# Rounding float64 weights block by block between the products that read them, in five VectorE passes instead of seven

## Chip, cores and metric

One core of one Trainium2 chip. The metric is the device time of one execution in microseconds (us).

## The reference, cut to what matters

Two steps follow each other. The first is a gated linear recurrence over 768 tokens for 4 batches of 8 heads of 48 channels. The second takes its output as `x` (4 x 768 x 384), mixes it with a two-dimensional Fourier transform, normalises it and sends it through a feed-forward layer whose weights arrive as float64.

```python
f = 1.0 / (1.0 + np.exp(-f_logit))
for t in range(S):
    state = f[:, :, t, :, None] * state + np.einsum('bhd,bhe->bhde', k[:, :, t], v[:, :, t])
    y[:, :, t] = np.einsum('bhd,bhde->bhe', q[:, :, t], state)
# ... x = y with the heads side by side: (B, S, H*D)
u = x + np.real(np.fft.fft(np.fft.fft(x, axis=1), axis=2))
un = (u - u.mean(-1)) / np.sqrt(u.var(-1) + 1e-06)        # shortened
return u + np.maximum(un @ w_ch1, 0.0) @ w_ch2            # w_ch1 384x1536, w_ch2 1536x384
```

## The kernel before

The attention runs in 16 units (two heads each, four units to a batch), the feed-forward layer in four batches of two halves. A unit's data lie in one of three buffers; its load into a buffer can only begin when the unit that held it is done. The float64 weights come as pairs of 32-bit words and are rounded to float32 on the chip, in 24 blocks of 128 x 384 (twelve of w1, twelve of w2), by integer arithmetic:

```python
def single(i, dst, src):                        # one block
    raw = p2.tile([128, n, 2], U32, tag="unT", name=f"raw{i}")
    # ... load; lo, hi are its two words; pow2, tail, tailf are three tiles of the pool ph1 (14 slots)
    vec.tensor_scalar(bits, hi, 3, 0x3FFFFFF8, ALU.logical_shift_left, ALU.bitwise_and)
    vec.scalar_tensor_tensor(bits, hi, 0xC0000000, bits, ALU.bitwise_and, ALU.bitwise_or)
    vec.scalar_tensor_tensor(bits, lo, 29, bits, ALU.logical_shift_right, ALU.bitwise_or)
    vec.tensor_scalar(tailb, lo, 0x1FFFFFFF, None, ALU.bitwise_and)
    vec.tensor_scalar(pow2b, bits, 0xFF800000, None, ALU.bitwise_and)
    nc.scalar.activation(tailf, tailb, AF.Copy, scale=2.0 ** -52)
    nc.gpsimd.tensor_tensor(tailf, tailf, pow2, ALU.mult)
    nc.gpsimd.tensor_tensor(dst, dst, tailf, ALU.add)
    vec.tensor_scalar(tailb, hi, 0x7FF00000, None, ALU.bitwise_and)
    vec.scalar_tensor_tensor(dst, tailb, float(897 << 20), dst, ALU.is_ge, ALU.mult)

# ... the states of a unit, in outputs(): one product and four dependent operations
nc.vector.tensor_tensor(st, ds, T.unsqueeze(2).to_broadcast([R, NCH - 1, D]), ALU.mult)
for c in range(1, NCH - 1):
    nc.vector.scalar_tensor_tensor(st[:, c], st[:, c - 1], T[:, c:c + 1], ds[:, c], ALU.mult, ALU.add)

# ... the feed-forward layer, in fnet(): the hidden activations take twelve of the 14 slots of ph1
for m in range(NF):                             # NF = 12
    for kt in range(3):
        nc.tensor.matmul(pp[:, :3 * 128], lhsT=w1[:, kt, m * 128:(m + 1) * 128], rhs=unT[:, kt], ...)
    h = ph1.tile([128, 3 * 128], F32, tag="h1", ...)
    nc.scalar.activation(h, pp[:, :3 * 128], AF.Relu)
for i in range(3):
    for m in range(NF):
        nc.tensor.matmul(po[:, :DM], lhsT=h1[m][:, i * 128:(i + 1) * 128], rhs=w2[:, m], ...)

# ... run(): at each tick every active unit goes one step on, then two steps of the work "behind" follow
run(attention, STEP, [weights()])               # the 24 blocks stand first in that work
```

Of the kernel before, what the change touches and what calls it, by code (L numbers as in the profile page):

```python
# [8 lines left out]
U32 = mybir.dt.uint32  # L9
# [8 lines left out]
HIGH = 22.0  # L18
X_MIN = -24.0
# [3 lines left out]
def kernel(  # L23
# [29 lines left out]
    p2 = ctx.enter_context(tc.tile_pool(name="p2", bufs=2))  # L53
    p3 = ctx.enter_context(tc.tile_pool(name="p3", bufs=4))
# [14 lines left out]
    deep = fixed([128, B * HP], "deep")  # L69
# [17 lines left out]
    for t in qkf_t:  # L87
        nc.vector.memset(t[32:64, 0:2], 0.0)
        nc.vector.memset(t[32:64, 2], 30.0)
# [7 lines left out]
    def load_unit(u):  # L97
        b, hp = divmod(u, HP)
        t = qkf_t[u % 3]
        for r in range(2):  # L100
            nc.sync.dma_start(out=t[ROWS[r]], in_=qkf[b, hp, r])
        vt = p3.tile([128, NCH, 2 * D], F32, tag="v", name=f"v{u}")
        nc.sync.dma_start(out=vt, in_=v[b, hp])
        return vt
# [9 lines left out]
    for t in at_t:  # L114
        nc.gpsimd.memset(t, 0.0)
# [4 lines left out]
    def single(i, dst, src):  # L120


        n = dst.shape[-1]
        raw = p2.tile([128, n, 2], U32, tag="unT", name=f"raw{i}")
        nc.sync.dma_start(out=raw.rearrange("p n w -> p (n w)"), in_=src)
        lo, hi = raw[:, :, 0], raw[:, :, 1]
        pow2 = ph1.tile([128, n], F32, tag="h1", name=f"pow2_{i}")
        tail = ph1.tile([128, n], F32, tag="h1", name=f"tail{i}")
        tailf = ph1.tile([128, n], F32, tag="h1", name=f"tailf{i}")
        bits, pow2b, tailb = (t.bitcast(U32) for t in (dst, pow2, tail))  # L130
        vec = nc.vector

        vec.tensor_scalar(bits, hi, 3, 0x3FFFFFF8, ALU.logical_shift_left, ALU.bitwise_and)
        vec.scalar_tensor_tensor(bits, hi, 0xC0000000, bits, ALU.bitwise_and, ALU.bitwise_or)
        vec.scalar_tensor_tensor(bits, lo, 29, bits, ALU.logical_shift_right, ALU.bitwise_or)

        vec.tensor_scalar(tailb, lo, 0x1FFFFFFF, None, ALU.bitwise_and)
        vec.tensor_scalar(pow2b, bits, 0xFF800000, None, ALU.bitwise_and)  # L138
        nc.scalar.activation(tailf, tailb, AF.Copy, scale=2.0 ** -52)  # L139
        nc.gpsimd.tensor_tensor(tailf, tailf, pow2, ALU.mult)  # L140
        nc.gpsimd.tensor_tensor(dst, dst, tailf, ALU.add)  # L141
        vec.tensor_scalar(tailb, hi, 0x7FF00000, None, ALU.bitwise_and)
        vec.scalar_tensor_tensor(dst, tailb, float(897 << 20), dst, ALU.is_ge, ALU.mult)  # L143

    def weights():
        pairs = [(w1[:, kt], w_ch1[kt * 128:(kt + 1) * 128]) for kt in range(3)]
        pairs += [(w2[:, m], w_ch2[m * 128:(m + 1) * 128]) for m in range(NF)]
        i = 0
        for dst, src in pairs:
            if src.dtype == F32:  # L150
                nc.sync.dma_start(out=dst, in_=src)
                yield
                continue
            words = src.bitcast(U32)
            for o in range(0, dst.shape[-1], 384):
                single(i, dst[:, o:o + 384], words[:, 2 * o:2 * (o + 384)])
                i += 1
                yield

    def attention(u, x_all):  # L160




        t = qkf_t[u % 3]
        Q, K, g = t[:R, 0], t[:R, 1], t[:R, 2]
        AT = at_t[u % 2]
        L = p2.tile([128, S], F32, tag="gk", name=f"L{u}")[:R]
        G = p2.tile([128, S], F32, tag="wq", name=f"G{u}")[:R]
        W = p2.tile([128, S], F32, tag="wk", name=f"W{u}")[:R]  # L170
        at = lambda a, i, c: a.rearrange("p (c t) -> p c t", t=C)[:, c, i]
        nc.vector.tensor_scalar(g, g, X_MIN, None, ALU.max)
        nc.scalar.activation(L, g, AF.Exp, scale=-1.0)
        nc.scalar.activation(L, L, AF.Ln, bias=1.0)  # L174
        nc.vector.tensor_tensor_scan(G, L, bound[:R], 0.0, ALU.add, ALU.min)  # L175
        nc.vector.tensor_reduce(deep[:R, u:u + 1], at(G, C - 1, slice(0, NCH)), mybir.AxisListType.X, ALU.max)

        T = p2.tile([128, NCH - 1], F32, tag="te", name=f"te{u}")[:R]
        nc.vector.tensor_tensor(T, at(G, C - 1, slice(0, NCH - 1)), at(L, 0, slice(1, NCH)), ALU.add)
        nc.scalar.activation(W, G, AF.Exp)  # L180
        nc.scalar.activation(G, G, AF.Exp, scale=-1.0)
        nc.scalar.activation(T, T, AF.Exp, scale=-1.0, bias=low[:R])
        nc.gpsimd.tensor_tensor(W, W, K, ALU.mult)  # L183
        nc.vector.tensor_tensor(Q, Q, G, ALU.mult)  # L184
        yield

        for h in range(2):
            ps = ps_a.tile([128, 2, 512], F32, tag="sc", name=f"sc{u}_{h}")
            for i in range(NCH // 2):
                o = (h * NCH // 2 + i) * C  # L190
                for s in range(2):
                    for r in range(2):
                        nc.tensor.matmul(ps[64 * s:64 * s + 64, r, i * C:(i + 1) * C],  # L193
                                         lhsT=W[ROWS[r], o + 64 * s:o + 64 * s + 64],
                                         rhs=Q[ROWS[r], o:o + C], start=True, stop=True)
            for r in range(2):
                half = slice(h * NCH // 2, (h + 1) * NCH // 2)
                nc.vector.copy_predicated(  # L198
                    AT[:, r, half],
                    causal.bitcast(U32).unsqueeze(1).to_broadcast([128, NCH // 2, C]),  # L200
                    ps[:, r, :NCH // 2 * C].rearrange("p (c t) -> p c t", t=C))
        yield
        yield from outputs(u, x_all, AT, Q, W, T, True)

    def attention_by_blocks(u, x_all):
# [25 lines left out]
        wq = p2.tile([128, S], F32, tag="wq", name=f"wq{u}")[:R]  # L231
        wk = p2.tile([128, S], F32, tag="wk", name=f"wk{u}")[:R]
        gk = p2.tile([128, S], F32, tag="gk", name=f"gk{u}")[:R]
# [89 lines left out]
        yield from outputs(u, x_all, AT, Q, K, T, False)  # L323

    def outputs(u, x_all, AT, Q, K, T, from_start):
# [12 lines left out]
        ds = ps[:R, 0, :(NCH - 1) * D].rearrange("p (c e) -> p c e", e=D)  # L338
        for c in range(NCH - 1):
            for r in range(2):  # L340
                nc.tensor.matmul(ds[FILL[r], c], lhsT=kT[:, c, FILL[r]], rhs=vt[:, c, r * D:(r + 1) * D],  # L341
                                 start=True, stop=True)
        st = p2.tile([128, NCH - 1, D], F32, tag="st", name=f"stt{u}")[:R]
        if from_start:
            nc.vector.tensor_tensor(st, ds, T.unsqueeze(2).to_broadcast([R, NCH - 1, D]), ALU.mult)
            ds = st
        else:
            nc.vector.tensor_copy(st[:, 0], ds[:, 0])
        for c in range(1, NCH - 1):
            nc.vector.scalar_tensor_tensor(st[:, c], st[:, c - 1], T[:, c:c + 1], ds[:, c],  # L350
                                           ALU.mult, ALU.add)
# [9 lines left out]
        for c in range(1, NCH):  # L361
            for r in range(2):
                nc.tensor.matmul(y[ROWS[r], c * C:(c + 1) * C], lhsT=st[ROWS[r], c - 1],  # L363
# [27 lines left out]
    def fnet(b, x):  # L391
# [42 lines left out]
        def mixed(name, rows, n):  # L434
            mix = ps_f.tile([128, 512], F32, tag="f", name=name)
            for T in range(3):
                nc.tensor.matmul(mix[:rows.stop - rows.start, :n], lhsT=zz[:, T, rows], rhs=cd[:, T, :n],  # L437
                                 start=(T == 0), stop=(T == 2))
            return mix

        mid = mixed(f"mid{b}", slice(HS, HS + 1), DM)
        row = p1.tile([128, DM], F32, tag="row", name=f"row{b}")
        nc.vector.tensor_tensor(row[0:1], mid[0:1, :DM], x[0:1, 3], ALU.add)
# [17 lines left out]
        for half in range(2):  # L461
# [11 lines left out]
            for m in range(NF):  # L473
                pp = ps_f.tile([128, 512], F32, tag="f", name=f"up{b}_{half}_{m}")
# [8 lines left out]
            for i in range(3):  # L483
                c = 3 * half + i
                po = ps_f.tile([128, 512], F32, tag="f", name=f"po{b}_{c}")
                for m in range(NF):
                    nc.tensor.matmul(po[:, :DM], lhsT=h1[m][:, i * 128:(i + 1) * 128], rhs=w2[:, m],  # L487
# [7 lines left out]
    def run(unit_of, step, behind):  # L495
        left, xs_of, active, done = [HP] * B, {}, [], 0
        u = tick = 0
        while u < B * HP or active or behind:
            if u < B * HP and tick % step == 0:
# [3 lines left out]
                active.append((b, unit_of(u, xs_of[b])))  # L503
                u += 1
            for b, unit in list(active):
                if next(unit, active) is active:
                    active.remove((b, unit))
                    left[b] -= 1
                    if not left[b]:
                        behind.append(fnet(b, xs_of.pop(b)))  # L510
# [5 lines left out]
    run(attention, STEP, [weights()])  # L516
# [3 lines left out]
    nc.vector.tensor_reduce(most[:R], deep[:R], mybir.AxisListType.X, ALU.max)  # L520
# [6 lines left out]
    with tc.If(again > 0):  # L527
        v_of.update({i: load_unit(i) for i in range(3)})
        run(attention_by_blocks, 3, [])
# [69 lines left out]
```

## Time and profile before

The median of the three runs taken first is 728.3 us (727.58 to 731.77). The profiled span is 725.6 us (that run read 727.62). I cut it at two places: where the first feed-forward product ("up") of the first batch starts, and where the second output product of that batch ("po_1") is added to x.

| stretch of before | us | TensorE busy | VectorE busy | GpSimd busy | mean clock |
|---|---|---|---|---|---|
| to the first up product | 205.4 | 109.1 | 163.2 | 89.2 | 0.69 |
| from there to the addition of po_1 | 45.9 | 45.9 | 15.8 | 9.9 | 0.98 |
| the rest | 474.3 | 449.8 | 93.4 | 34.1 | 0.98 |

The row of the first stretch is one line of the view by windows; its columns are the window, its length, then busy us and count for PE, PEld, DVE, ACT and POOL, then the clock, the DMA share and GB/s:

```profile
0.00:205.40 205.40, 109.14 (x1044) 73.52 (x1044) 163.23 (x320) 63.14 (x111) 89.23 (x78) 0.69 0.47 118
```

VectorE is 79% busy here.

### The profile page before, as it was taken

The page shows a single profiled execution, that of the slowest core. Times are in us where ns is not written, and L with a number is a line of the kernel's source. Part 1 is how long each engine was busy: PE and PEld are TensorE (multiplying, and loading weights), DVE is VectorE, ACT ScalarE, POOL GpSimd, SP SyncE. Part 2 cuts the span into 40 slices and gives each one's busy share as a digit, 9 for nine tenths or more (in the row PEclk, how much of TensorE's full clock was granted, in tenths as well). Part 3 has the DMA queues.
Part 4 walks back from the last instruction along what each step waited for, and adds up shares of the span by engine and source line. Part 5 has one row for each costly group of instructions (what it writes and reads, how often), then busy time and mean ns, then how long its engine had stood idle before and what let it go on. Part 6 is the DMA issues. An engine that isn't in the chain of part 4 may idle for free.

```text
span 725.6 us, 8305 instructions
## 1 busy us (share of the span) xinstructions
PE 604.9 (83%) x3402; PEld 370.1 (51%) x3402; DVE 272.5 (38%) x541; ACT 167.7 (23%) x317; POOL 133.2 (18%) x109
## 2 busy tenths in 40 slices
PE   0853446157799999999999999987999998999995
PEld 0642334034456665666556655554555553555553
DVE  5777788888861421126922100144000004001000
ACT  2521322124261132122531120122202101210200
POOL 3225545644220400021400000120000010000001
PEclk9875555659789999999999999997999999899999
DMA  9835444242320030313310000000000000000000
GB/s 169 225 85 130 127 105 129 85 114 82 65 50 1 23 77 1 77 39 74 67 25 11 23 0 12 22 1 1 0 23 11 1 22 11 1 0 33 0 12 27
DMA packets 11182, 35.56 MB, mean 49 GB/s; under 512 B 1600, under 2 KB 3776, under 8 KB 9472
## 3 DMA queue, kind: packets, MB, share of 16 engines
q1 hardware_dynamic: 10368, 32.58, 18.1%
q0 software_dynamic: 768, 2.36, 0.8%
q8 instruction: 29, 0.48, 0.3%
q14 instruction: 17, 0.14, 0.1%
HBM read 30.22 MB, written 4.72 MB: 48 GB/s over the span
## 4 chain that ended last, share of the span: by engine, by line
PE 49%; DVE 4%; ACT 1%; DMA 1%; POOL 1%; issue 0%; ACTq 0%; DVEq 0%; POOLq 0%
PE up L476 20%; PE po L487 19%; PE z L424 3%; PE pt L469 1%; PE y L363 1%; PE y L358 1%; PE mix L437 1%; PE sc L193 1%; DVE bs L453 1%; DMA out_dram<-x,place 1%; PE mid L437 1%; PE ds L341 1%; POOL eo L400 1%; PE st L334 1%; PE yt L374 0%
## 5 line engine op out<-in xcount | busy, mean ns | idle before, releaser
L476 PE MATMUL up<-unT,w 128*128 128x384 f32 x576 | 195.3, 500 | 2.3 <-ACT unT L470 2.3
L487 PE MATMUL po<-w,h 128*128 128x384 f32 x576 | 188.8, 487 | 0.0
L476 PEld LDWEIGHTS up<-unT,w 128*128 128x128 f32 x576 | 111.2, 195 | 81.7 <-issue 5.8
L487 PEld LDWEIGHTS po<-w,h 128*128 128x128 f32 x576 | 108.9, 190 | 75.1 <-issue 0.5
L489 DVE TENSOR_TENSOR x<-po,x 128x384 f32<-128x384 f32 x24 | 13.4, 558 | 292.0 <-PE po L487 292.0
L479 ACT ACTIVATE h<-up 128x384 f32<-128x384 f32 x96 | 47.0, 490 | 136.3 <-PE up L476 136.3
L386 POOL DMA_INDIRECT out_dram<-x,place x12 | 13.1, 1090 | 331.3 <-DVE x L489 324.5
L363 PE MATMUL y<-qkf,stt 48*48 48x128 f32 x320 | 34.2, 325 | 46.7 <-DVE stt L350 36.4
L193 PE MATMUL sc<-qkf,W 48*64 48x128 f32 x768 | 39.1, 336 | 32.9 <-DVE qkf L184 24.2
L183 POOL TENSOR_TENSOR W<-W,qkf 112x768 f32<-112x768 f32 x16 | 29.9, 1866 | 117.2 <-ACT W L180 117.2
L193 PEld LDWEIGHTS sc<-qkf,W 48*64 48x64 f32 x768 | 31.7, 170 | 37.3 <-issue 20.5
L363 PEld LDWEIGHTS y<-qkf,stt 48*48 48x48 f32 x320 | 17.2, 134 | 62.5 <-DVE stt L350 45.0
L140 POOL TENSOR_TENSOR tailf<-tailf,pow 128x384 f32<-128x384 f32 x24 | 35.6, 1485 | 70.7 <-DVE pow L138 40.5
L358 PE MATMUL y<-at,v 128*64 128x128 f32 (+1 forms) x384 | 37.2, 315 | 8.9 <-ACT tailf L139 5.9
L198 DVE COPY_PREDICATED at<-causal,sc 128x384 f32<-128x384 uint32 x64 | 33.9, 579 | 28.3 <-PE sc L193 28.3
L358 PEld LDWEIGHTS y<-at,v 128*48 128x48 f32 (+1 forms) x384 | 26.4, 149 | 18.5 <-issue 6.9
L175 DVE TENSOR_TENSOR_SCAN G<-L,bound 112x768 f32<-112x768 f32 x16 | 28.6, 1786 | 14.4 <-ACT L L174 14.4
L437 PE MATMUL mix<-cd,zz 128*128 128x385 f32 x72 | 26.9, 521 | 1.9 <-DVE x L447 1.9
L350 DVE SCALAR_TENSOR_TENSOR stt<-stt,te 112x48 f32<-112x48 f32 x64 | 27.5, 429 | 1.1
L143 DVE SCALAR_TENSOR_TENSOR w<-tail,w 128x384 f32<-128x384 uint32 x24 | 19.7, 822 | 21.6 <-POOL w L141 21.6
L141 POOL TENSOR_TENSOR w<-w,tailf 128x384 f32<-128x384 f32 x24 | 27.0, 1126 | 1.9
L426 ACT COPY zz<-z 128x386 f32<-128x386 f32 x12 | 5.8, 482 | 82.5 <-PE z L424 82.5
(77 smaller groups left out, 512.5 us busy)
## 6 DMA issues: line engine op xcount, KB each, us to landing
qkf<-in_qkf_dram SPq DMA_DIRECT2D x32, 432.0 KB, 5.8
raw<-in_w_ch_dram SPq DMA_DIRECT2D x24, 384.0 KB, 3.4
v<-in_v_dram SPq DMA_DIRECT2D x16, 288.0 KB, 3.5
out_dram<-x SPq DMA_DIRECT2D x12, 192.0 KB, 1.8
tab<-in_seq_tab_dram SPq DMA_DIRECT2D x1, 1158.0 KB, 15.6
cd<-in_dim_tab_dram SPq DMA_DIRECT2D x1, 576.0 KB, 18.0
out_dram<-x,place POOLq DMA_INDIRECT x12, 2.5
masks<-in_sel_dram SPq DMA_DIRECT2D x1, 64.0 KB, 5.7
```

Of the source, the lines that this page charges most:

```text
L140: nc.gpsimd.tensor_tensor(tailf, tailf, pow2, ALU.mult)
L175: nc.vector.tensor_tensor_scan(G, L, bound[:R], 0.0, ALU.add, ALU.min)
L183: nc.gpsimd.tensor_tensor(W, W, K, ALU.mult)
L193: nc.tensor.matmul(ps[64 * s:64 * s + 64, r, i * C:(i + 1) * C], lhsT=W[ROWS[r], o + 64 * s:o + 64 * s + 64], rhs=Q[ROWS[r], o:o + C], sta ...
L198: nc.vector.copy_predicated(AT[:, r, half], causal.bitcast(U32).unsqueeze(1).to_broadcast([128, NCH // 2, C]), ps[:, r, :NCH // 2 * C].rea ...
L350: nc.vector.scalar_tensor_tensor(st[:, c], st[:, c - 1], T[:, c:c + 1], ds[:, c], ALU.mult, ALU.add)
L358: nc.tensor.matmul(y[FILL[r], c * C:(c + 1) * C], lhsT=vt[:, c, r * D:r * D + (64 if r == 0 else D)], rhs=AT[:, r, c], start=(c % 4 == 0), ...
L363: nc.tensor.matmul(y[ROWS[r], c * C:(c + 1) * C], lhsT=st[ROWS[r], c - 1], rhs=Q[ROWS[r], c * C:(c + 1) * C], start=False, stop=True, skip ...
L437: nc.tensor.matmul(mix[:rows.stop - rows.start, :n], lhsT=zz[:, T, rows], rhs=cd[:, T, :n], start=(T == 0), stop=(T == 2))
L476: nc.tensor.matmul(pp[:, :3 * 128], lhsT=w1[:, kt, m * 128:(m + 1) * 128], rhs=unT[:, kt], start=(kt == 0), stop=(kt == 2))
L479: nc.scalar.activation(h, pp[:, :3 * 128], AF.Relu)
L487: nc.tensor.matmul(po[:, :DM], lhsT=h1[m][:, i * 128:(i + 1) * 128], rhs=w2[:, m], start=(m == 0), stop=(m == NF - 1))
```

## The change

The intent: round each block right in front of the products that read it, so that the first batch's feed-forward layer need not wait for all 24 blocks; need two VectorE passes less and only two scratch slots at a time; run the states as one scan; send the first batch's units ahead.

```diff
+SMALLEST = 1.125 * 2.0 ** -15
-    def single(i, dst, src):
+    def single(dst, src):
...
+        nc.scalar.activation(size, hi.bitcast(F32), AF.Abs)
         vec.tensor_scalar(bits, hi, 3, 0x3FFFFFF8, ALU.logical_shift_left, ALU.bitwise_and)
         vec.scalar_tensor_tensor(bits, hi, 0xC0000000, bits, ALU.bitwise_and, ALU.bitwise_or)
-        vec.scalar_tensor_tensor(bits, lo, 29, bits, ALU.logical_shift_right, ALU.bitwise_or)
-        vec.tensor_scalar(tailb, lo, 0x1FFFFFFF, None, ALU.bitwise_and)
+        vec.tensor_scalar(tailb, lo, 1, None, ALU.logical_shift_right)
+        vec.scalar_tensor_tensor(dst, size, SMALLEST, dst, ALU.is_ge, ALU.mult)
         vec.tensor_scalar(pow2b, bits, 0xFF800000, None, ALU.bitwise_and)
-        nc.scalar.activation(tailf, tailb, AF.Copy, scale=2.0 ** -52)
-        nc.gpsimd.tensor_tensor(tailf, tailf, pow2, ALU.mult)
-        nc.gpsimd.tensor_tensor(dst, dst, tailf, ALU.add)
-        vec.tensor_scalar(tailb, hi, 0x7FF00000, None, ALU.bitwise_and)
-        vec.scalar_tensor_tensor(dst, tailb, float(897 << 20), dst, ALU.is_ge, ALU.mult)
+        nc.scalar.activation(tail, tailb, AF.Copy, scale=2.0 ** -51)
+        nc.gpsimd.tensor_tensor(tail, tail, pow2, ALU.mult)
+        nc.gpsimd.tensor_tensor(dst, dst, tail, ALU.add)
...  (states, in the order channel, chunk; te has a zero column between channels)
-            nc.vector.tensor_tensor(st, ds, T.unsqueeze(2).to_broadcast([R, NCH - 1, D]), ALU.mult)
+            nc.vector.tensor_tensor_scan(flat(st[:R]), ps[:R, 0, :NCH * D], flat(te), 0.0, ALU.add, ALU.mult)
...  (feed-forward)
             for m in range(NF):
+                if first and half == 0 and m % 3 == 0:
+                    for kt in range(3):
+                        weights(w1[:, kt], w_ch1[kt * 128:(kt + 1) * 128], slice(m * 128, (m + 3) * 128))
...
                 for m in range(NF):
+                    if first and c == 0:
+                        weights(w2[:, m], w_ch2[m * 128:(m + 1) * 128])
...
-            if u < B * HP and tick % step == 0:
+            if u < B * HP and (u < 3 or u - 3 in done) and (first and u < HP or tick % step == 0):
...
-    run(attention, STEP, [weights()])
+    run(attention, STEP, True)
```

Left out: the masked copies of two heads merged into one, g worked on in place instead of in tiles L and G, `mid` with fewer columns and products, one pad memset moved to GpSimd, the raw words of a block in a pool of their own, the two halves of a unit loaded in the other order.

## The prediction

> **What bounds the kernel now.** I read the page's slices first, then busy time by windows, the groups by line, and two stretches of the timeline. In the slices one digit is a tenth of busy time in 18.1 us:
>
> ```profile
> PE   0853446157799999999999999987999998999995
> DVE  5777788888861421126922100144000004001000
> POOL 3225545644220400021400000120000010000001
> PEclk9875555659789999999999999997999999899999
> ```
>
> There are two stages. For the first eleven slices (about 205 us) TensorE is half idle at about half clock and VectorE is the fullest engine; after that TensorE is full to the end. The first feed-forward product marks the border, in the view of one line (min/median/max ns, then first to last start):
>
> ```profile
> L476 PE MATMUL up<-unT,w x576: 486/486/1006, 205.4 to 693.6; 128*128 128x384 f32 x192
> ```
>
> By windows (stretch, length, then busy us and count for PE, PEld, DVE, ACT, POOL; clock, DMA share, GB/s), one window of each stage:
>
> ```profile
> 120.00:140.00 20.00, 7.25 (x65) 5.00 (x65) 18.78 (x33) 5.68 (x9) 11.96 (x10) 0.67 0.37 110
> 680.00:700.00 20.00, 20.00 (x63) 11.78 (x62) 0.00 (x0) 3.93 (x8) 0.00 (x0) 1.00 0.00 0
> ```
>
> So the late stage is pure matmul time that the change barely touches; what can be won is the first 205 us. What fills VectorE and GpSimd there, by groups (busy us, mean ns | idle before, releaser):
>
> ```profile
> L140 POOL TENSOR_TENSOR tailf<-tailf,pow 128x384 f32<-128x384 f32 x24 | 35.6, 1485 | 70.7 <-DVE pow L138 40.5 <-ACT tailf L139 25.4 <-DVE w L134 4.8
> L141 POOL TENSOR_TENSOR w<-w,tailf 128x384 f32<-128x384 f32 x24 | 27.0, 1126 | 1.9
> L143 DVE SCALAR_TENSOR_TENSOR w<-tail,w 128x384 f32<-128x384 uint32 x24 | 19.7, 822 | 21.6 <-POOL w L141 21.6
> L350 DVE SCALAR_TENSOR_TENSOR stt<-stt,te 112x48 f32<-112x48 f32 x64 | 27.5, 429 | 1.1
> L175 DVE TENSOR_TENSOR_SCAN G<-L,bound 112x768 f32<-112x768 f32 x16 | 28.6, 1786 | 14.4 <-ACT L L174 14.4
> ```
>
> The weight rounding (L133 to L143) is seven VectorE passes and two GpSimd passes on each of 24 blocks. Means of the seven: 0.46+0.55+0.66+0.42+0.35+0.53+0.82 = 3.8 us, or 91 us of VectorE. Its timeline shows why 0.82 is not 0.56 (start, us, engine):
>
> ```profile
> 140.86 0.55 DVE L134 SCALAR_TENSOR_TENSOR w<-raw,w 128x384 uint32<-128x384 uint32 x1
> 141.08 1.91 POOL L140 TENSOR_TENSOR tailf<-tailf,pow 128x384 f32<-128x384 f32 x1 [2.40 <-DVE pow L138]
> 141.33 0.35 DVE L142 TENSOR_SCALAR tail<-raw 128x384 uint32<-128x384 uint32 x1
> 141.59 0.55 DVE L135 SCALAR_TENSOR_TENSOR w<-raw,w 128x384 uint32<-128x384 uint32 x1
> 143.07 0.99 POOL L141 TENSOR_TENSOR w<-w,tailf 128x384 f32<-128x384 f32 x1
> ```
>
> GpSimd's product took 1.91 us instead of the 0.99 its twin takes with VectorE quiet: it ends 0.85 us after VectorE's last pass, as if it had only begun then.
>
> **What the Trainium skill says.** "SBUF — State Buffer", section "Who interferes with whom": a VectorE instruction in a two-port mode, or with two SBUF inputs, and a GpSimd instruction that reads SBUF exclude one another for the whole instruction. The trace agrees: 1.91 against 0.99 above. I therefore count VectorE's weight passes and GpSimd's as one serial resource. "TensorE: Matmul & The Clock Gate", section "What's actually happening": the clock is halved by default and released by sustained activity. The trace agrees: clock 0.50 in the window 60 to 80 us, 1.00 when full. "Advanced Engine Details and Errata", section "PSUM Cachelines": a non-contiguous PSUM pattern slows matmuls significantly. No row of before has the new pattern; it is a risk below.
>
> **The change, part by part.**
>
> *Where the weights stand.* Before, blocks are issued two a tick among the attention units; all 24 are rounded before the first feed-forward product. The changed program as built has three blocks whole and two begun before that product; the others come between the products of the first batch: w1 three blocks ahead of every three m, w2 one block ahead of each product of po_0. The same attention work stands ahead of the first product in both (scores of units 0 to 7 or 8, and the first batch's transform). So the border moves forward by the VectorE time of some 20 blocks.
>
> *Stage A, to the first product.* I counted the changed program's VectorE queue up to there and priced it with the means of before: eight to nine units' first halves at 0.60 (clamp) + 0.2 (copy) + 1.79 (scan) + 0.2 + 1.15 (Q product) = 3.9, together 34; sixteen merged predicated copies at 2 x 0.54 = 1.08 (four of 0.58 become two of twice the size), 17; seven state scans of 288 elements at 1786 x 288/768 = 0.67, say 0.72, 5; the blocks, 9; memsets 4; the transform's additions, statistics and normalisation, 14. Sum 84 us, against 161 of busy time in the windows before to 205 us, 79%; 84/0.79 = 106, a little high, because durations overlap at their ends and busy time does not. Walked by dependency (three unit buffers, 7 us of loading and 17 us of chain, so some 8 us a unit) I get 100 to 104. I take **103 us**.
>
> *Stage B1, nine w1 blocks, three to four units, half a batch of up.* VectorE's queue: 47 us by the same means. TensorE and VectorE now wait for each other in program order (up waits for blocks, a unit's scores stand behind up, the predicated copy waits for the scores), so I allow 70% busy: **68 us**, to 171.
>
> *Stage B2, twelve w2 blocks.* Here I expect a new wait. The three scratch tiles of a block come from the same 14 slots as the hidden activations, of which twelve are live until po_2 has read them: two slots remain, so block i+1 cannot write its tail before GpSimd has finished block i. In VectorE's queue a block is: tail, compare, power, then the next block's first two passes; start to start 0.27+0.47+0.27+0.27+0.47, with the last one's end 1.85 us. Then GpSimd 1.0 + 1.0 and some 0.2 of handovers: **4.05 us a block, 49 us** for twelve, to about 221 with the last product. In this time TensorE has only po_0 and po_1, 24 products of two records at 0.32: 15.5 us. It will be two thirds idle.
>
> *Stage C, the rest, TensorE bound.* Costs per record from full-clock stretches of the chain:
>
> ```profile
> 573.72 23.22 PE po L487 x72
> 550.23 23.49 PE up L476 x72
> 596.94 8.13 PE z L424 x28
> 605.07 2.03 PE mid L437 x6
> 607.10 6.04 PE mix L437 x18
> ```
>
> A batch: z 8.1, mix 6.0, transposes 2.4, two halves of 23.5+23.2, and mid, which falls from six records of 384 columns to four of 193, 2.03 x (4 x 193)/(6 x 384) = 0.7: 110.6 us. Left after po_1: po_2 7.7, the first batch's second half 47.5, three batches 332, and 5.4 units at some 5.9 (full-clock pieces near 391 to 409 us: 0.6+0.5+0.7+1.45+1.1+1.5) with the two small added products, 33. Sum 420. Before, from 321 us to the end the same count gives 362 of work in 404 elapsed, so 42 of gaps, cold clock at batch borders and tail, and these borders stay; with 2 more for the second half, 44.
>
> *State scan.* One scan replaces a product and four dependent operations: 0.40 + 4 x 0.43 = 2.1 us to 0.7 of VectorE, 16 times 22 us in all. About half lies in stage A and B, where it is already counted; the other half lies under full TensorE time and is worth little.
>
> Sum: 103 + 68 + 50 + 420 + 44 = 685 us of span; runs read some 2 to 3 us above the span (728.3 against 725.6), while A and B1 are rounded up. I predict **684 us**, 6% faster.
>
> **Rivals.** (1) *GpSimd and VectorE, serialised by few slots, eat most of the gain.* If a w2 block costs 5.5 us and B1 runs at 55% busy, 18 + 18 us are added: about 720, within 2%. For it: GpSimd's L140 averages 1.49, not 1.0, before. Against it: in B2 hardly anything but the blocks runs. (2) *The new layouts slow TensorE.* The increments are written to PSUM at a stride of six and the states loaded at that stride as weights. If these loads (L363, 134 ns) and products (L341, 0.23 us) doubled, a unit would take 1 to 2 us more, 6 to 10 us over the units of stage C: about 692. (3) *TensorE was waiting for the attention chain, not for the weights.* Then stage A would shrink little. Against it: unit 0 and unit 1, before any block is rounded, stand 11 us apart (scores at 16.7 and 28.1), later ones 23 to 34 with the blocks among them (67.1, 93.7, 116.7, 151.0). (4) *Better overlap than I allow:* A in 92, B1 in 58, gaps 38: about 660.
>
> **Range and chances.** A and B1 carry about 12 us of doubt each way, B2 8, C 8; added as independent, 20; rival 1 lengthens the upper side. Range 661 to 711. Two per cent faster is below 713.7: chance 0.92; same 0.06; slower 0.02, which would need a stall that I do not see.
>
> **What would show it.** Right: first up product near 103 us; last first-half up product near 171; twelve w2 blocks about 4 us apart, with VectorE's tail pass released by GpSimd, TensorE below 40% busy and the clock down there; po_2 starting near 220; 460 us from there to the end. Wrong: a first up product after 130 (A), blocks much further apart than 4 us (B2), unit products with longer records than before (rival 2), or more than 50 us of gaps after po_1, because fewer attention units are left to fill the batch borders.

## More of the kernel before

What the queue of loads waits for in the first 80 us shows who holds it up (us in all, times, longest):

```profile
SPq L125 <- DVE tail L142: 42.6, 6, 11.5
SPq L101 <- PE y L363: 11.6, 1, 11.6
```

It waits for the rounding first (L125 loads a block of weights) and only a quarter as long for a unit buffer (L101 loads a unit).

## The result and the profile after

The changed kernel is correct. Its median is 707.66 us (705.66 to 711.25, four runs), against 729.71 us (727.58 to 731.77, four runs) for the kernel before on the same chip. A ratio here is the mean time of one kernel's fast runs over that of the other's of the same rounds, so not quite the ratio of the two medians: 0.9703 (95% interval 0.9652 to 0.9755), 3.0% faster. The range of the prediction held it and the direction was right, but the gain is 22 us where 44 were forecast.

The page's slices, of 17.65 us each now:

```profile
PE   0777898775765799997999999978999997999995
...
DVE  3767786885577500039403110152000005000000
...
POOL 4231541465455400112300101020000010000001
PEclk9997899988786799998999999997999999899999
```

The half idle stretch now lasts fourteen slices (247 us), three more than before, only less idle. The two places of the cut, and the end of the first half's up products, give four stages, which by windows read:

```profile
0.00:118.50 118.50, 79.63 (x1015) 61.89 (x1015) 83.15 (x120) 54.41 (x91) 43.20 (x50) 0.92 0.65 136
```

```profile
118.50:195.30 76.80, 55.68 (x402) 32.45 (x404) 49.60 (x69) 28.55 (x53) 38.20 (x28) 0.82 0.38 93
195.30:243.90 48.60, 30.73 (x109) 14.75 (x109) 33.98 (x63) 14.90 (x27) 27.43 (x25) 0.75 0.27 81
243.90:706.00 462.10, 433.32 (x1937) 261.91 (x1937) 80.37 (x146) 84.41 (x170) 29.82 (x27) 0.97 0.07 18
```

| stage | predicted us | measured us | difference |
|---|---|---|---|
| A, to the first up product | 103 | 118.5 | +15.5 |
| B1, to the last up product of the first half | 68 | 76.8 | +8.8 |
| B2, to the addition of po_1 | 50 | 48.6 | -1.4 |
| C, the rest | 464 | 462.1 | -1.9 |
| sum | 685 | 706.0 | +21.0 |

So the whole error lies in A and B1. Note VectorE's busy time in A: 83 us, where the prediction had counted 84. The busy time was right; it filled 70% of the stage and not 79%.

What the up products and the load queue wait for. The first two lines are the view of the up products (min/median/max ns, first to last start; then us and times of waiting, weight loads included), the other two are the load queue's first 80 us:

```profile
L479 PE MATMUL up<-unT,w x576: 486/486/1008, 118.5 to 673.8; 128*128 128x384 f32 x192
...
  POOL w L146: 42.8, 15
```

```profile
SPq L106 <- PE y L356: 23.4, 2, 17.8
SPq L104 <- PE y L361: 20.6, 5, 9.3
```

Up products now wait for GpSimd's last pass of a block. The 42.8 us count most waits twice, once for the weight load (23.0) and once for the product (19.8); TensorE itself stood still some 20 us. The load queue waits for the last products of a unit (L104 loads a unit, L106 its v): the wait for the rounding in that queue became a wait for unit buffers. In the time line the fourth unit of the first batch shows it: its load is issued at 35.05, when unit 0 is done, and VectorE takes it up 8 us later.

```profile
35.05 0.79 SPq L104 DMA_DIRECT2D qkf<-in_qkf_dram  x2
...
43.07 0.56 DVE L164 TENSOR_SCALAR qkf<-qkf 112x768 f32<-112x768 f32 x1 [1.89 <-DMA qkf<-in_qkf_dram]
```

The groups of GpSimd's two passes and of the new state scan (busy us, mean ns | idle before):

```profile
L145 POOL TENSOR_TENSOR tail<-tail,pow 128x384 f32<-128x384 f32 x24 | 32.6, 1360 | 48.4 <-DVE pow L142 47.8 <-ACT size L136 0.4
L146 POOL TENSOR_TENSOR w<-w,tail 128x384 f32<-128x384 f32 x24 | 31.5, 1311 | 1.8
```

```profile
L344 DVE TENSOR_TENSOR_SCAN stt<-ds,te 112x288 f32<-112x288 f32 x16 | 12.1, 754 | 44.0 <-PE ds L341 44.0
```

And one steady w2 block in stage B2, out of the time line (start, us, engine):

```profile
227.86 0.36 DVE L140 TENSOR_SCALAR tail<-raw 128x384 uint32<-128x384 uint32 x1 [0.89 <-POOL w L146]
...
228.14 0.55 DVE L141 SCALAR_TENSOR_TENSOR w<-size,w 128x384 f32<-128x384 f32 x1
...
228.72 0.36 DVE L142 TENSOR_SCALAR pow<-w 128x384 uint32<-128x384 uint32 x1
229.00 0.35 DVE L138 TENSOR_SCALAR w<-raw 128x384 uint32<-128x384 uint32 x1
229.23 0.99 POOL L145 TENSOR_TENSOR tail<-tail,pow 128x384 f32<-128x384 f32 x1 [1.40 <-DVE pow L142]
229.39 1.25 DVE L139 SCALAR_TENSOR_TENSOR w<-raw,w 128x384 uint32<-128x384 uint32 x1
...
230.30 1.19 POOL L146 TENSOR_TENSOR w<-w,tail 128x384 f32<-128x384 f32 x1
231.52 0.36 DVE L140 TENSOR_SCALAR tail<-raw 128x384 uint32<-128x384 uint32 x1 [0.88 <-POOL w L146]
```

A block takes 3.66 us. VectorE's next tail pass waits 0.88 us for GpSimd's addition, as forecast. L139, which takes 0.55 us elsewhere, takes 1.25 us beside GpSimd's product: this is what the prediction calls exclusion, one engine's instruction standing still until the other's is done.

### The profile page after: what moved, and what is told of

It reads as the page before. It is cut to its first block, busy times and chain, and to the rows that moved or that the text cites. A ratio compares the mean times of both kernels' runs of the same rounds, so it can differ in the third digit from the quotient of the medians.

```text
span 706.0 us, 8313 instructions
## 1 busy us (share of the span) xinstructions
PE 599.4 (85%) x3458; PEld 371.0 (53%) x3458; DVE 247.1 (35%) x398; ACT 182.3 (26%) x341; POOL 138.7 (20%) x130
## 4 chain that ended last, share of the span: by engine, by line
PE 67%; DVE 15%; POOL 8%; issue 4%; ACT 4%; DMA 2%; POOLq 0%; ACTq 0%; DVEq 0%
PE up L479 27%; PE po L492 24%; POOL tail L145 3%; POOL w L146 3%; PE z L422 3%; PE mix L435 3%; DVE at L192 2%; DVE w L141 2%; DVE qkf L170 2%; PE y L356 2%; PE sc L188 2%; DVE pow L142 2%; PE ds L335 1%; DMA qkf<-in_qkf_dram 1%; PE pt L469 1%
## 5 line engine op out<-in xcount | busy, mean ns | idle before, releaser
L479 PE MATMUL up<-unT,w 128*128 128x384 f32 x576 | 205.8, 518 | 22.6 <-POOL w L146 19.8
L492 PE MATMUL po<-w,h 128*128 128x384 f32 x576 | 198.0, 502 | 16.7 <-POOL w L146 16.7
L192 DVE COPY_PREDICATED at<-causal,sc 128x768 f32<-128x768 uint32 x32 | 32.5, 1032 | 38.0 <-PE sc L188 38.0
L188 PEld LDWEIGHTS sc<-qkf,W 48*64 48x64 f32 x768 | 28.4, 155 | 31.9 <-POOL W L178 21.2
L145 POOL TENSOR_TENSOR tail<-tail,pow 128x384 f32<-128x384 f32 x24 | 32.6, 1360 | 48.4 <-DVE pow L142 47.8
L146 POOL TENSOR_TENSOR w<-w,tail 128x384 f32<-128x384 f32 x24 | 31.5, 1311 | 1.8
L356 PEld LDWEIGHTS y<-at,v 128*64 128x64 f32 (+1 forms) x384 | 25.4, 147 | 9.3 <-issue 5.5
L170 DVE TENSOR_TENSOR_SCAN qkf<-qkf,bound 112x768 f32<-112x768 f32 x16 | 28.1, 1755 | 0.4
L344 DVE TENSOR_TENSOR_SCAN stt<-ds,te 112x288 f32<-112x288 f32 x16 | 12.1, 754 | 44.0 <-PE ds L341 44.0
L470 ACT COPY unT<-pt 128x384 f32<-128x384 f32 x24 | 11.1, 478 | 61.8 <-PE pt L469 61.8
L469 PE MATMUL pt<-ident,un 128*128 128x128 f32 x72 | 13.7, 323 | 14.9 <-DVE mv L454 9.9
L361 PE MATMUL y<-qkf,stt 48*48 48x128 f32 x320 | 22.7, 288 | 4.2 <-DVE stt L344 4.1
```

Of the source, the lines that this page charges most:

```text
L145: nc.gpsimd.tensor_tensor(tail, tail, pow2, ALU.mult)
L146: nc.gpsimd.tensor_tensor(dst, dst, tail, ALU.add)
L170: nc.vector.tensor_tensor_scan(g, g, bound[:R], 0.0, ALU.add, ALU.min)
L188: nc.tensor.matmul(ps[64 * s:64 * s + 64, r, i * C:(i + 1) * C], lhsT=W[ROWS[r], o + 64 * s:o + 64 * s + 64], rhs=Q[ROWS[r], o:o + C], sta ...
L192: nc.vector.copy_predicated(AT[:, :, half], causal.bitcast(U32).unsqueeze(1).unsqueeze(1).to_broadcast([128, 2, NCH // 2, C]), ps[:, :, :N ...
L356: nc.tensor.matmul(y[FILL[r], c * C:(c + 1) * C], lhsT=vt[:, c, r * D:r * D + (64 if r == 0 else D)], rhs=AT[:, r, c], start=(c % 4 == 0), ...
```

## The experiments

Each kernel is the changed one with one edit, if not said otherwise, timed over three rounds against the kernel before on the same chip. In the table the ratio is to before; the spans are those of the profiled execution, cut as above (B is B1 and B2 together). The difference is that of the ratios times 728 us.

| kernel | median us | ratio to before (95%) | to the changed kernel, us | A | B | C |
|---|---|---|---|---|---|---|
| before | 728.3 | 1 | | 205.4 | 45.9 | 474.3 |
| changed | 707.66 | 0.9703 (0.9652 to 0.9755) | 0 | 118.5 | 125.4 | 462.1 |
| e_place | 691.94 | 0.9500 (0.9464 to 0.9537) | -15 | 172.4 | 42.4 | 475.4 |
| e_two (wrong results) | 651.80 | 0.8943 (0.8906 to 0.8979) | -55 | 119.4 | 48.9 | 484.4 |
| e_nogp (wrong results) | 669.51 | 0.9185 (0.9163 to 0.9207) | -38 | 120.9 | 84.9 | 462.3 |
| e_vec | 684.35 | 0.9411 (0.9374 to 0.9449) | -21 | 113.3 | 104.5 | 462.7 |
| e_slots | 711.24 | 0.9753 (0.9720 to 0.9786) | +4 | 120.6 | 127.6 | 464.5 |
| e_order | 705.97 | 0.9714 (0.9653 to 0.9775) | +1 | 119.1 | 121.1 | 460.7 |
| e_pad | 706.23 | 0.9689 (0.9665 to 0.9712) | -1 | 119.6 | 123.8 | 464.2 |
| e_q4 | 696.94 | 0.9566 (0.9543 to 0.9590) | -10 | 110.3 | 127.8 | 456.9 |
| e_w1first | 695.41 | 0.9546 (0.9520 to 0.9572) | -11 | 116.5 | 111.9 | 464.4 |
| e_oldscan | 706.55 | 0.9702 (0.9666 to 0.9737) | 0 | 123.0 | 115.9 | 463.9 |
| f_q4vec | 668.46 | 0.9198 (0.9148 to 0.9248) | -37 | 106.1 | 104.7 | 455.2 |
| f_all | 674.69 | 0.9257 (0.9226 to 0.9288) | -32 | 106.6 | 111.1 | 455.6 |

The two halves of B do not compare as cleanly as the whole: the built program shifts unit work from one stretch into the next.

Stage C differs mainly by how many of the 16 units are left for it: 13 have passed their gate scan before the border in the changed kernel, 11 in e_place (C 13 us longer), 10 in e_two (22 us longer), so some 7 us a unit.

### What did the new placement bring?

**e_place**: the five passes stay, but all blocks are issued ahead of the first batch, as in the kernel before.

```diff
+    def all_weights():      # w1 by kt and columns, then w2 by m, one block a step
-                if first and half == 0 and m % 3 == 0: ... weights(w1 ...)
-                    if first and c == 0: weights(w2 ...)
-    behind = []
+    behind = [all_weights()] if first else []
```

> The changed kernel with the placement alone undone: the five new passes stay, but all 24 blocks are issued two a tick among the attention units, before the first batch's transform and products, as in the kernel before. Theory (what gained is the cheaper rounding and the state scan; the placement between the products lost some of it, because TensorE, VectorE and GpSimd then wait for each other in program order): first up product near 165 us, no stretch of products waiting for blocks behind it, everything after it at the pace of the TensorE bound stage; span 675 to 695, so 12 us or more faster than the changed kernel. Rival (the placement itself gained, as I predicted): first up near 165 to 175 and span of 715 or more, at least 8 us slower than the changed kernel.

Measured: 692 us, 15 us faster than the changed kernel. The first up product comes 54 us later, but stage B is 83 us shorter, because its products wait for no block; two more units left for stage C cost 13 us of that. So the placement, on which the prediction built its stages, costs 15 us as built; what gains is the rest of the change (the five passes, the first batch's units sent ahead and the smaller parts), 36 us from before to e_place. Which of these gains was not separated. In two windows of e_place VectorE and GpSimd are both nearly full at the same time:

```profile
100.00:120.00 20.00, 4.55 (x85) 4.09 (x81) 20.00 (x29) 8.27 (x15) 19.20 (x13) 0.59 0.45 124
120.00:140.00 20.00, 16.80 (x159) 11.20 (x152) 18.80 (x32) 9.95 (x19) 19.77 (x10) 0.81 0.59 154
```

In the changed kernel's stage B1 VectorE is 65% busy and GpSimd 50%. These full rows are not all work: the time an engine is held up by the other lies inside its instructions. GpSimd's two passes average 1.62 and 1.69 us in e_place, against 0.99 undisturbed. The opposite, the old seven passes at the new place, was not measured: they hold three scratch slots at once, where only two are left. My build of it ended in a deadlock.

### What does a block still cost, and on which engine?

**e_two**: only the first two bit passes are left of a block, so the weights are wrong.

```diff
-        nc.scalar.activation(size, hi.bitcast(F32), AF.Abs)
-        vec.tensor_scalar(tailb, ...); vec.scalar_tensor_tensor(dst, size, ...); vec.tensor_scalar(pow2b, ...)
-        nc.scalar.activation(tail, ...); nc.gpsimd.tensor_tensor(tail, ...); nc.gpsimd.tensor_tensor(dst, ...)
```

> Wrong results on purpose: of the rounding of a block only the first two bit passes on VectorE are left; the pass on ScalarE, the three others on VectorE and both on GpSimd are gone. It measures what the rounding still costs in the changed kernel. Theory (rounding is the bound of both feed-forward stretches of the first batch): the twelve w2 blocks go from 42 to about 16 us, the stretch from the first up to the last first-half up from 77 to about 50, stage A loses 3 to 8 us; run near 650. Rival (the chain of the attention units and their three buffers limits the middle stretch, not the blocks): only the w2 stretch falls, the middle stretch stays above 65, run near 676.

Measured: 651.8 us, where the rival said 676, so the rival is out: what is long after stage A is made by the blocks and not by the chain of the units. The stretch B1 fell to 25.6 us, lower even than expected, but partly because unit work left it: the ninth unit's scores come at 158.5 us, behind the stretch, where in the changed kernel three units' scores (126.6, 146.5, 184.3) lie within it. The w2 stretch (B2) fell to 23.3 us, not to 16. Stage A did not become shorter (119.4 us). This run has a stall there, from the first batch's transform, that the changed kernel does not have: an addition of VectorE that took 1.34 us in the changed kernel (at 72.14) took 5.18 us here beside GpSimd's product and subtraction. It may hide up to 3.8 us. e_nogp below has no such stall (1.35 us), and its stage A is 120.9 us, so GpSimd's part of the rounding is not what made A long, and all of the rounding a few us at most.

```profile
71.33 1.82 POOL L166 TENSOR_TENSOR W<-W,qkf 112x768 f32<-112x768 f32 x1 [0.76 <-POOL deep L160]
...
71.75 5.18 DVE L385 TENSOR_TENSOR eo<-x 128x1152 f32<-128x1152 f32 x1 [0.47 <-ACT x L361]
73.11 2.62 POOL L386 TENSOR_TENSOR eo<-x 128x1152 f32<-128x1152 f32 x1
```

**e_nogp**: the two GpSimd passes are left out, so the weights are wrong; the seven passes of the other engines stay.

```diff
-        nc.gpsimd.tensor_tensor(tail, tail, pow2, ALU.mult)
-        nc.gpsimd.tensor_tensor(dst, dst, tail, ALU.add)
```

> Wrong results on purpose: the two GpSimd passes of a block are left out, the five VectorE passes and the two ScalarE passes stay. Together with the run without any of them but two (651.8 us) it splits the price of the rounding. Theory (GpSimd's passes and the exclusion between GpSimd and VectorE carry most of it): w2 blocks 2.1 us apart instead of 3.66, the middle stretch near 50 us instead of 77, the run near 665. Rival (VectorE's passes and the detour over ScalarE carry it): blocks 2.9 us apart or more, the run 682 or more, no better than the run with VectorE doing these two passes itself (684.4).

Measured: 669.5 us; B1 takes 49 us (120.9 to 169.9). Two passes on an engine that is half idle carry 38 of the 55 us that a rounding without the rest would save; three VectorE passes and two ScalarE passes carry 18 once those two are gone (in the other order the shares may differ). The spacing of w2 blocks could not be read as one number: unit work lies between them, and their tail passes stand 2.2 to 6.2 us apart.

**e_vec**: VectorE does these two passes itself. Results are right.

```diff
-        nc.gpsimd.tensor_tensor(tail, tail, pow2, ALU.mult)
-        nc.gpsimd.tensor_tensor(dst, dst, tail, ALU.add)
+        vec.tensor_tensor(tail, tail, pow2, ALU.mult)
+        vec.tensor_tensor(dst, dst, tail, ALU.add)
```

> The last product and the last addition of the rounding are done by VectorE instead of GpSimd. Theory (in the w2 stretch a block is one serial chain over VectorE, ScalarE and GpSimd because two scratch slots are left and the two engines exclude each other; GpSimd's two passes of 1.0 us and their handovers are the larger part): spacing of w2 blocks from 3.66 to about 2.8 us, that stretch 10 us shorter; the middle stretch some 5 us shorter too as GpSimd's waits of 4 us vanish; run near 692. Rival (VectorE is the bound, its extra 0.8 us a block comes on top): spacing 3.7 or more and run 5 us slower, near 713.

Measured: 684.4 us, 21 us faster with more work on the engine that was thought to be the bound. B1 fell from 76.8 to 65.6 us. The blocks of w2 stand 2.83 us apart, and no pass is stretched; each takes 0.35 or 0.55 us:

```profile
195.12 0.55 DVE L145 TENSOR_TENSOR tail<-tail,pow 128x384 f32<-128x384 f32 x1
195.59 0.55 DVE L139 SCALAR_TENSOR_TENSOR w<-raw,w 128x384 uint32<-128x384 uint32 x1
196.06 0.55 DVE L146 TENSOR_TENSOR w<-w,tail 128x384 f32<-128x384 f32 x1
```

**e_slots**: 16 slots instead of 14 in the pool of hidden activations and scratch tiles.

```diff
-    ph1 = ctx.enter_context(tc.tile_pool(name="ph1", bufs=14))
+    ph1 = ctx.enter_context(tc.tile_pool(name="ph1", bufs=16))
```

> The changed kernel with 16 instead of 14 slots for the hidden activations and the scratch tiles, so that four slots and not two are left in the w2 stretch. My prediction put its block time of 4.05 us down to the two slots and to the exclusion of VectorE and GpSimd together. Theory (exclusion alone is enough): the blocks still stand 3.3 us or more apart, VectorE passes and GpSimd passes stretch each other when they overlap, the run at most 5 us faster than the changed kernel. Rival (the two slots are the wait): blocks 2.8 us apart or less, w2 stretch 10 us shorter, run 10 us faster or more.

Measured: 711.2 us, not faster at all, and blocks 3.75 us apart (3.66 in the changed kernel). The tail pass L140 no longer waits for the slot; it begins at once and takes 1.17 us instead of 0.36, ending 0.2 us after GpSimd's product:

```profile
228.12 1.00 POOL L145 TENSOR_TENSOR tail<-tail,pow 128x384 f32<-128x384 f32 x1 [1.69 <-DVE pow L142]
228.16 1.17 DVE L140 TENSOR_SCALAR tail<-raw 128x384 uint32<-128x384 uint32 x1
229.19 0.99 POOL L146 TENSOR_TENSOR w<-w,tail 128x384 f32<-128x384 f32 x1
229.25 1.35 DVE L139 SCALAR_TENSOR_TENSOR w<-raw,w 128x384 uint32<-128x384 uint32 x1
```

So the wait for the slot, which the profile names, only covered the exclusion of the two engines. With it gone, the same time shows as longer passes. The 3.75 us are nearly the sum of both engines: 1.75 us of VectorE's five passes, start to start as the prediction priced them, and twice 0.99 us of GpSimd's.

### Why was stage A late?

**e_order**: the two halves of a unit are loaded in the old order.

```diff
-        for r in (1, 0):
+        for r in range(2):
```

> The changed kernel with one line put back: each unit loads its first half before its second, as in the kernel before. Theory: in the changed kernel unit 0 starts at 13.13 us instead of 8.87 because its second half waits for a memset and stands behind unit 1's load; stage A carries this delay to its end, so here the scores of unit 0 come at about 17 (21.2 in the changed kernel), the first up product near 114 (118.5), and the run is 4 us faster, about 703.5. Rival: the start is absorbed by the three unit buffers or the rounding of the weights, whose clock is set by VectorE and GpSimd; then the first up product stays within 1.5 us of 118.5 and the time within 1 us of 707.5.

Measured: no difference (ratio 0.9714), and this run decided nothing. Unit 0's scores still came at 21.05 us: the scheduler had built the same load queue from the other source order.

**e_pad**: the pad memset of the third row goes back to VectorE, with which the built load queue has both halves of unit 0 at its head.

```diff
-        nc.gpsimd.memset(t[32:64, 2], 30.0)
+        nc.vector.memset(t[32:64, 2], 30.0)
```

> The changed kernel with one memset moved back from GpSimd to VectorE (the pad of the third row of a unit buffer), which in the built program puts the two halves of unit 0 back together at the head of the load queue, as before. In the run that turned the order of the halves in the source (e_order) the built queue was the same as in the changed kernel, and unit 0's scores came at 21.05 us, so that run did not test the start. Theory (the late start is carried through stage A): scores of unit 0 near 17, first up product near 114.5, run 3 to 4 us faster than the changed kernel, about 704. Rival (absorbed by the wait for the unit buffers or by the blocks): first up product within 1.5 us of 118.5, run within 1.5 us.

Measured: unit 0's scores come at 16.89 us, 4.3 us earlier, unit 1's at 27.96 (28.97 in the changed kernel), unit 2's at 38.06 (37.95), and the first up product at 119.6. The head start is gone by the third unit. My theory falls and the rival holds: the late start is not the cause.

**e_q4**: a fourth unit buffer. Two small tiles get one buffer instead of two, and one shares another's, to make room.

```diff
-    qkf_t = [fixed([128, 3, S], f"qkf{i}") for i in range(3)]
+    qkf_t = [fixed([128, 3, S], f"qkf{i}") for i in range(4)]
...   (u % 3 becomes u % 4, u + 3 becomes u + 4, u - 3 in done becomes u - 4 in done; v_of[3] is loaded at the start)
```

> The changed kernel with four unit buffers instead of three, so that the whole first batch can be loaded at once (room made by single buffers for two small tiles). In the changed kernel unit 3's load is issued at 35.05, when unit 0 is done, and its scores come at 54.3, 16 us after unit 2's. Theory (stage A is long because the fourth unit waits for a buffer, not because of the rounding): unit 3's scores near 46, first up product near 110, run about 8 us faster, near 700. Rival (stage A is set by the work of VectorE and its waits, whoever brings the data): first up within 2 us of 118.5, run within 2 us of the changed kernel.

Measured: 10 us faster, the first up product at 110.3 us, and unit 3's scores at 47.85 us (54.3 in the changed kernel). VectorE takes unit 3 up at 37.17, without a wait for its data. This confirms the theory: 8 us of stage A were the wait for a buffer, first the fourth unit's.

### Does the program order between the engines cost in stage B1?

**e_w1first**: all twelve w1 blocks are issued ahead of the first up product.

```diff
-                if first and half == 0 and m % 3 == 0:
-                    for kt in range(3):
-                        weights(w1[:, kt], w_ch1[kt * 128:(kt + 1) * 128], slice(m * 128, (m + 3) * 128))
+                if first and half == 0 and m == 0:
+                    for o in range(0, DFF, 384):
+                        for kt in range(3):
+                            weights(w1[:, kt], w_ch1[kt * 128:(kt + 1) * 128], slice(o, o + 384))
```

> The changed kernel with the twelve w1 blocks all issued in front of the first up product of the first batch, not three by three between them; w2 stays between the products of po_0. Theory (the middle stretch is long because TensorE, VectorE and GpSimd wait for each other in program order: up waits for a block, a unit's scores stand behind up, the masked copy behind the scores, the next block's passes behind the copy): first up near 145, but the middle stretch falls from 77 to 35 us or less; the run 10 to 18 us faster, 690 to 698. Rival (the middle stretch is simply the work of nine blocks on VectorE and GpSimd): what the middle stretch loses, stage A gains; run within 4 us of the changed kernel.

Measured: 11 us faster, as the theory said, but not in the way it said. The first up product stayed where it was (116.5; it needs only the first three blocks), and from there to the last up product of the half it takes 53 us (76.8). Two up products run at once; the others start at 148.0, after the first two activations, which come at 145.7, behind passes of blocks and units in ScalarE's queue. From then on no up product waits for GpSimd. Part of the gain is shifted: only one unit's scores (132.1) lie in this stretch, where the changed kernel has three. The w2 stretch gave back part of the gain: 54 us from the first product of po_0 to the addition of po_1, where the changed kernel takes 44 (200.1 to 243.9).

### Is the state scan worth anything?

**e_oldscan**: one product and four dependent operations again, in the new layout.

```diff
-            nc.vector.tensor_tensor_scan(flat(st[:R]), ps[:R, 0, :NCH * D], flat(te), 0.0, ALU.add, ALU.mult)
+            nc.vector.tensor_tensor(st[:R, :, n], ds[:R, :, n], te[:, :, n], ALU.mult)
+            for c in range(1, NCH - 1):
+                nc.vector.scalar_tensor_tensor(st[:R, :, c], st[:R, :, c - 1], te[:, 0, c:c + 1], st[:R, :, c],
+                                               ALU.mult, ALU.add)
...   (n is slice(0, NCH - 1); the two small added products are left out)
```

> The changed kernel with the running sum of the states undone: one product and four dependent operations on VectorE instead of one scan, the two small added products gone, same layouts. It puts back some 1.4 us of VectorE time per unit, 22 us in all. Theory (as predicted, it lies on the path while VectorE and the unit chain set the pace, for 11 to 13 of the 16 units before the border, and is hidden after it): run 5 to 11 us slower than the changed kernel, near 715. Rival (stage A waits for unit buffers and the later stretches for GpSimd, so VectorE has room): within 2.5 us of the changed kernel.

Measured: no difference in time (ratio 0.9702 against 0.9703). The rival holds. Stage A is 4.5 us longer without the scan, stage B 9.5 us shorter; why B gains was not tested. By the durations the scan saves 21.7 us of VectorE (33.8 against 12.1), of busy time 13.2, and the run gains nothing from it.

### A version that beats both

**f_q4vec** is e_q4 and e_vec together.

> Four unit buffers and VectorE doing the last product and addition of the rounding, together. Alone they gave about 10 and 23 us. Theory (they act on different stretches, the first on stage A, the second on the two stretches after it): the gains add, first up product near 105, run near 675. Rival (both shorten the same waits in stage A, where the second alone had moved the first up product from 118.5 to 113.3): first up near 110, run 680 or more.

Measured: 668.5 us, ratio 0.9198 to before; 37 us faster than the changed kernel, somewhat more than the 31 that the two gave alone. The first up product comes at 106.1 us.

**f_all** is that and e_w1first together.

> Four unit buffers, VectorE doing the last product and addition, and all twelve w1 blocks issued in front of the first up product. Theory (program order between TensorE and VectorE still costs in the middle stretch when GpSimd is out of it): 5 us or more faster than the same without the last part, 670 or less. Rival (with GpSimd out, the middle stretch is VectorE's work and its order does not matter): within 3 us of the run with the other two.

Measured: 674.7 us, 4 us slower than f_q4vec by the ratios (their intervals overlap, but its fastest run, 674.1 us, is no faster than the slowest of f_q4vec, 674.07). The theory is refuted for the run as a whole: with GpSimd out of the blocks the order of the w1 blocks brings nothing. B1 alone is still 10 us shorter (55.8 against 66.1), but B2 is 17 us longer (55.3 against 38.7), because unit work moved into it: the tenth unit's scores come at 166.2, not at 144.7. Not tried were e_place's placement with four buffers or with VectorE doing all passes.

## Why the prediction was right and wrong, step by step

- **Stage A, 103 us, was too short by 15.5.** The count of VectorE's busy time was right (84 us predicted, though its own terms add to 83; 83.15 in the window). The two steps that turned it into a time failed. The share of 79% was taken from a stage in which the load queue waited for the rounding; without those blocks the stage is bounded by something else, and VectorE was 70% busy. The walk by dependency, "so some 8 us a unit", was the mis-sized term: the first scores of the eight units that stand ahead come at 21.2 to 109.3 us, 12.6 us apart. Unit 0's chain took 21.8 us from its first VectorE pass to the end of its last product, not 17, and those of the first seven units took 20 to 31 us (in the kernel before unit 0's took 19.0). With the mean of these seven, 24.8, and the 8.0 us from load to first pass, the same walk gives an estimate of 10.9 us a unit, not 8. e_two's chains, almost without rounding, are as long (18 to 33), so what lengthens them is not the blocks; it stays open. Of the 15.5 us, the missing buffer carries 8.2 (e_q4), and together with GpSimd's passes, 12.4 (f_q4vec: 106.1 us). Why the second part helps A is not settled: e_vec alone has it at 113.3 us, but the two runs that leave these passes out altogether have it at 119.4 and 120.9. The late first load, 4.3 us, carries nothing (e_pad). The last 3 us stay open.
- **B1, 68 us, was too short by 8.8.** The prediction had 47 us of VectorE work at 70% busy; the window shows 49.6 at 65%. The step that failed is that GpSimd's passes were allowed for in B2 alone: over all blocks they averaged 1.36 and 1.31 us, not 1.0, and TensorE waited some 20 us for them here. With VectorE doing them B1 takes 65.6 us, without them 49, without most of the rounding 25.6. The trace shows the exclusion in this stretch: a pass of GpSimd took 4.05 us while VectorE ran one pass after another, and ended 0.85 us after the last of them.

```profile
171.63 4.05 POOL L145 TENSOR_TENSOR tail<-tail,pow 128x384 f32<-128x384 f32 x1 [3.35 <-DVE pow L142]
174.24 0.59 DVE L139 SCALAR_TENSOR_TENSOR w<-raw,w 128x384 uint32<-128x384 uint32 x1
```

How much of the 8.8 us is this exclusion, and how much GpSimd's longer passes and the handovers to it, no run separates. That the engines wait for each other in program order adds to it (e_w1first), but without GpSimd in the blocks the whole run gains nothing from another order (f_all).
- **B2, 50 us, was right (48.6), by a mechanism that was half right and with some luck.** The wait shown for a slot is real, but it is not what sets the pace: four slots leave a block at 3.75 us. The exclusion does. The predicted 4.05 us was too high (3.66 measured), and 4.8 us pass before the first product of po_0, which the prediction did not have: 4.8 + 43.8 happens to come near its 50. TensorE was 63% busy there (30.7 of 48.6 us, at a mean clock of 0.75), not under 40%: unit work lay in this stretch too.
- **C, 464 us, was right (462.1).** Its two terms, 420 of work at full clock and 44 of gaps and slow clock, were not measured apart; TensorE was busy 433.3 us.
- **The state scan** was put at 22 us of VectorE, half of it of use. Its duration was nearly right (0.754 us, 0.72 predicted), its use was nil (e_oldscan).
- **The rivals.** Rival 1 (the exclusion eats the gain) came nearest; it sat in B1 and not in B2, where the blocks are 3.66 us apart and not 5.5. Rival 2 (slower layouts) did not come about: the increments' products have the same durations as before, and the loads of states as weights grew by 37 ns each at the median, whose cost no run tests. Rival 3 (TensorE was waiting for the attention chain, not for the weights) was dismissed on two intervals between units, 11 us against 23 to 34. The first units say little, though: units 0 to 2 (scores at 16.7, 28.2 and 37.4) have their buffers from the start, and only later ones wait for one. The old trace already shows that wait, 11.6 us. Once the blocks are out of the way, the chain and its buffers are the next bound, as e_q4's 8.2 us and the stage A of e_two and e_nogp show, which is no shorter.
- **What the prediction never asked** is what the old placement would give with the new passes. That is the larger part of the result: e_place at 692 us. The border between the stages moved forward by 86.9 us, and stage B, which had been 45.9 us, grew by 79.5. The prediction also called the first stage's clock about half; it averaged 0.69 in the kernel before.

## What to carry to other kernels

When a bound is taken out of a stage, the busy share of the old stage says nothing of the new one: walk the next resource in line (here the buffers that let data in) and give it its measured time per unit. VectorE and GpSimd held each other up here, so in the rounding they count as one engine (3.75 us a block in e_slots, nearly the sum of both). Moving work onto the busier of the two was a gain (e_vec, 21 us), and more buffers between them only turned a wait into a longer instruction (e_slots). Issuing work just in time between the products that need it can put its latency on the path of the busiest engine; measure it against issuing all of it ahead (e_place, 15 us).

## What the Trainium skill lacked or had wrong

- "SBUF — State Buffer", section "Who interferes with whom", has the rule, and these traces agree with it, but not how it looks in a trace: the blocked time is inside the duration of the instruction, without a wait. A 128 x 384 pass took 1.17 us instead of 0.36 beside GpSimd's product of 1.00 us (e_slots), and a 128 x 1152 addition 5.18 instead of 1.34 (e_two).
- "Perfetto Trace Analysis", section "Optimization Strategy", says that the same gap repeating can mean too few buffers. Here the gap (0.88 us a block, on VectorE) did come from a slot, but with two more slots the block took 3.75 us, where it had taken 3.66. That a gap can hide an exclusion is not said there.
- "Advanced Engine Details and Errata", section "PSUM Cachelines", says that any non-contiguous pattern slows matmuls significantly. Increments of 48 float32 columns written at a stride of six elements took as long as contiguous ones in these float32 products (min/median/max ns; the first line is the kernel before, the second the changed one):

```profile
L341 PE MATMUL ds<-v,kT x320: 206/222/340, 22.0 to 477.3; 128*64 128x48 f32 x97, 128*48 128x48 f32 x63
```

```profile
L335 PE MATMUL ds<-v,kT x320: 206/222/342, 27.8 to 461.4; 128*64 128x48 f32 x100, 128*48 128x48 f32 x60
```

- No page that I read gives the price of a strided weight load: with the states at a stride of six elements its median went from 120 to 157 ns (320 loads of 48 x 48).
